# Softmax denominators of 16 attention units by GpSimd, masks by one f16 matmul term in seven units, and a new order of all steps

## The chip, the cores and the metric

The kernel runs on one core of one Trainium2 chip. The metric is the device time of one launch in microseconds (us); lower is better. Five engines work side by side, each through its own instructions in program order: TensorE (PE) multiplies matrices, VectorE (DVE) and ScalarE (ACT) do elementwise work, GpSimd (POOL) does elementwise work and reductions over partitions, and SyncE (SP) starts the transfers between main memory and the on-chip memory. An instruction that waits for another engine holds up everything behind it on its own engine.

## What is computed

Banded attention with block summaries, and then a two-layer MLP with GELU, in float32 (the MLP's weights come as float64). Cut to what matters:

```python
B, H, S, D = 4, 8, 768, 64;  block, window = 32, 16
k_sum = k.reshape(B, H, 24, 32, D).max(axis=3)
v_sum = v.reshape(B, H, 24, 32, D).mean(axis=3)
scores_l = where(|i - j| < window, q @ k.T / 8, -1e9)
scores_s = q @ k_sum.T / 8 + log(block)
a = softmax(concat([scores_l, scores_s]))
x = a @ concat([v, v_sum])                     # 3072 rows x 512
out = gelu(x @ w_in) @ w_out                   # 512 -> 2048 -> 512
```

## The kernel before

**Precision.** A matmul operand is split into two float16 halves, high and low (`..._hi` steps make the high half, `..._lo` steps the rest), and each product is made of three f16 matmuls: high·high, high·low, low·high.

**Tiling.** Attention is cut into 24 units, each 256 queries of four heads of one batch. A unit's scores stand with keys (64 band keys, 24 block summaries, 32 more band keys) on the partitions and 4 × 256 queries along the free axis, a tile of 128 × 1024. Two units (all eight heads) give one chunk of 256 rows for the MLP, 12 chunks in all. Chunks 0 to 3 run the first layer plainly (`phase1 c i`, 24 matmuls of 256 columns). Chunks 4 to 11 go in pairs with a seven-product scheme of Strassen's kind (`sx_...` and `t_...` prepare the sums of its operands, `product p j m` are the matmuls, `keep` and `h_add` combine them). `gelu`, `g_hi`, `g_lo` and then `phase2 c i` (12 matmuls of 512 columns each), `store` and `put` finish a chunk.

**One unit, step by step.** `load_q`, `load_k`, `load_v`, `load_vs` (transfers; `s_load_vs` is a copy on ACT), splits of q, k and v, `scores` (48 small matmuls into `ps_s`), then one of two ways to mask: units 0 to 3 first put the mask into `ps_s` by matmul (`f_mask`, line 617: two terms, f16 mask times a scaled unit matrix, for each half of 512 columns, so 4 matmuls) and copy the scores out on ACT (`evac`, line 654); units 4 to 23 add an f32 mask on DVE while copying (`add_mask`, line 657). Then `maximum` (POOL, line 665, a reduction over the partitions of 128 × 1024), `shift` (DVE), `exponent` (ACT), the split of the probabilities (`s_p_hi` or `p_hi`, then `p_lo`), and `values` on PE: first the denominators, a matrix of ones times the high and the low half of the probabilities (line 709, four matmuls of 512 columns, written side by side into two halves of the partitions), then 48 small matmuls (line 718). `norm_den` (ACT) copies the denominators, `norm_take`, `norm_rec`, `norm_spread` (DVE) invert them, `norm_mult` scales, `x_hi` and `x_lo` (or the `sx` steps) split the result for the MLP.

**Other steps named below.** `wi_diff` and `v_diff` get the low half of a part of `w_in` or of v on PE (an f32 matmul with a unit matrix, recorded as two, lines 424 and 698, and an f16 one, lines 425 and 699), and `wi_dlo` and `v_dlo` copy it out on ACT; `wi_lo` and `v_lo` get the same on DVE. `wi_bits` and `wo_bits` turn float64 bits into float32 on DVE. `warm k n` (line 778) are n filler matmuls whose result nobody reads. `prep_k` and `prep_v` form the block summaries on DVE.

**Order.** The order of everything is written out by hand in `ORDER`, a list of some 1,500 steps, with each engine's program being the steps that it executes, in that order. The waits between engines follow from the data. So where a step stands in `ORDER` sets what it can hold up: transfers are all issued from SP in the order of the list.

**Buffers.** `ps_s` and `ps_v` are single PSUM tiles, four more PSUM banks rotate. `p_h`, `p_l` and `m32` (the maxima) are single; `s32`, `q32` and `v32` are double (unit u uses number u mod 2). `den0` holds the denominators of units 0 to 7 and serves further units in turn with three more tiles.

Of the kernel before, what the change touches and what calls it, by code (L numbers as in the profile page):

```python
# [74 lines left out]
wi_bits 2 0, k_lo 2, wi_dlo 0 1, evac 1, exponent 0, maximum 1, s_p_hi 0, s_k_hi 3, sum_vt 0, sum_vt 1, sum_vt 2,
mean_vt, f_mask 2, scores 2, shift 1, p_lo 0, wi_bits 2 1, wi_bits 1 0, wi_bits 2 2, wi_bits 1 1, k_lo 3, wi_bits 1 2,
s_load_vs 0, v_hi 0, load_vs 1, v_diff 0 1, v_diff 0 0, evac 2, v_hi 1, v_dlo 0 0, v_dlo 0 1, exponent 1, wi_hi 2 1,
wi_hi 2 0, v_diff 1 1, f_mask 3, values 0, wi_diff 2 0, v_diff 1 0, norm_den 0, load_v 2, load_q 3, load_q 4,
s_load_vs 2, q_hi 3, s_p_hi 1, v_hi 2, norm_take 0, norm_rec 0, norm_spread 0, norm_mult 0, p_lo 1, fetch_w_in 6,
load_v 3, v_dlo 1 0, fetch_w_in 5, fetch_w_in 3, wi_hi 1 1, wi_hi 1 0, v_dlo 1 1, warm 3 2, v_diff 2 0, wi_bits 6 0,  # L80
q_lo 3, wi_bits 6 1, wi_diff 1 1, wi_dlo 1 1, v_dlo 2 0, x_hi 0, s_load_vs 3, maximum 2, wi_bits 6 2, x_lo 0, shift 2,
wi_bits 5 0, values 1, v_diff 2 1, scores 3, wi_diff 2 1, wi_dlo 2 0, v_dlo 2 1, evac 3, wi_diff 1 0, wi_hi 6 1,
norm_den 1, v_hi 3, wi_diff 6 1, wi_dlo 1 0, wi_dlo 2 1, norm_take 1, norm_rec 1, norm_spread 1, norm_mult 1,
v_diff 3 0, v_dlo 3 0, wi_hi 6 0, x_hi 1, v_diff 3 1, wi_diff 6 0, exponent 2, wi_dlo 6 0, wi_bits 3 0, x_lo 1,
phase1 0 0, phase1 0 1, fetch_w_in 4, s_p_hi 2, maximum 3, s_k_hi 5, s_k_hi 4, wi_bits 4 0, shift 3, wi_bits 4 1,
p_lo 2, wi_bits 5 1, wi_bits 4 2, wi_bits 3 1, values 2, wi_dlo 6 1, exponent 3, gelu 0 0, norm_den 2, phase1 0 2,
phase1 0 6, s_p_hi 3, s_q_hi 4, wi_bits 5 2, norm_take 2, wi_bits 3 2, norm_rec 2, wi_hi 4 0, gelu 0 2, wi_diff 4 0,
p_lo 3, norm_spread 2, wi_hi 5 1, wi_hi 5 0, g_hi 0 0, wi_hi 3 1, v_dlo 3 1, g_lo 0 0, load_v 5, fetch_w_out 0,
wo_bits 0 0, load_q 5, fetch_w_in 7, load_v 4, norm_mult 2, wo_bits 0 1, wo_bits 0 2, fetch_w_out 4, gelu 0 1,
wi_bits 7 0, g_hi 0 2, wi_dlo 4 0, wi_hi 3 0, wi_hi 4 1, wi_diff 5 0, gelu 0 6, wi_dlo 5 0, wi_diff 3 1, wi_diff 4 1,  # L90
wi_diff 5 1, wi_diff 3 0, x_hi 2, wi_dlo 3 0, wi_dlo 4 1, wi_bits 7 1, x_lo 2, values 3, wi_dlo 3 1, phase1 0 3,
phase1 0 4, norm_den 3, wo_hi 0, wi_dlo 5 1, wi_bits 7 2, phase1 0 5, norm_take 3, s_load_vs 4, wo_lo 0, norm_rec 3,
norm_spread 3, g_lo 0 2, wo_bits 4 0, norm_mult 3, k_lo 4, gelu 0 4, gelu 0 3, x_hi 3, x_lo 3, g_hi 0 3, wi_hi 7 0,
v_hi 4, wo_bits 4 1, wo_bits 4 2, g_hi 0 6, wo_hi 4, k_lo 5, g_lo 0 3, q_lo 4, g_hi 0 1, gelu 0 5, g_lo 0 1, wo_lo 4,
fetch_w_out 1, s_load_vs 5, wi_lo 7 0, wo_bits 1 0, phase1 1 2, phase1 1 1, phase1 1 6, gelu 1 1, g_hi 0 5, wi_hi 7 1,
g_hi 1 1, wo_bits 1 1, scores 4, phase1 1 0, wo_bits 1 2, g_lo 0 5, g_lo 1 1, wo_hi 1, wo_lo 1, wi_lo 7 1, v_hi 5,
fetch_w_out 2, gelu 1 6, g_hi 1 6, gelu 1 0, g_hi 1 0, g_hi 0 4, wo_bits 2 0, g_lo 1 6, wo_bits 2 1, wo_bits 2 2,
phase1 1 5, phase1 1 3, s_q_hi 5, wo_hi 2, v_lo 5, g_lo 1 0, g_lo 0 6, wo_lo 2, fetch_w_out 3, load_mask, gelu 1 5,
gelu 1 3, gelu 1 2, g_hi 1 3, wo_bits 3 0, phase1 1 7, phase1 0 7, phase1 1 4, phase2 1 1, wo_bits 3 1, g_lo 0 4,
wo_bits 3 2, g_hi 1 2, g_lo 1 2, q_lo 5, gelu 1 4, wo_hi 3, load_v 7, load_q 6, s_q_hi 6, fetch_w_out 5, fetch_k 1 0,  # L100
wo_lo 3, wo_bits 5 0, g_lo 1 3, q_lo 6, wo_bits 5 1, wo_bits 5 2, gelu 0 7, gelu 1 7, g_hi 1 5, g_hi 1 4, g_hi 0 7,
wo_hi 5, add_mask 4, maximum 4, wo_lo 5, prep_k 1 0, g_lo 1 4, load_q 7, fetch_w_out 6, wo_bits 6 0, wo_bits 6 1,
fetch_w_out 7, wo_bits 6 2, wo_hi 6, shift 4, exponent 4, wo_lo 6, v_lo 4, load_v 6, wo_bits 7 0, g_lo 0 7,
wo_bits 7 1, phase2 0 1, phase2 1 0, phase2 0 3, phase2 1 2, phase2 0 0, phase2 0 2, phase2 0 4, phase2 0 5, scores 5,
s_p_hi 4, wo_bits 7 2, p_lo 4, wo_hi 7, wo_lo 7, values 4, phase2 0 6, norm_den 4, g_hi 1 7, store 0 0, fetch_v 1 0,
fetch_k 1 1, load_q 8, load_k 6, add_mask 5, g_lo 1 5, maximum 5, prep_v 1 0, norm_take 4, prep_k 1 1, shift 5,
load_k 7, s_k_hi 6, s_k_hi 7, g_lo 1 7, norm_rec 4, prep_k_end 1 0, k_lo 6, norm_spread 4, exponent 5, s_p_hi 5,
put 0 0, fetch_v 1 1, q_hi 7, p_lo 5, prep_k_end 1 1, norm_mult 4, k_lo 7, phase2 1 3, phase2 1 4, phase2 0 7,
store 0 1, phase2 1 5, k_sums 1 0, x_hi 4, scores 6, values 5, prep_v 1 1, x_lo 4, norm_den 5, k_sums 1 1, phase2 1 6,
phase2 1 7, add_mask 6, norm_take 5, norm_rec 5, norm_spread 5, norm_mult 5, load_k 8, fetch_v 3 0, s_q_hi 8,  # L110
s_k_hi 8, maximum 6, q_lo 8, load_vs 6, put 0 1, x_hi 5, store 1 0, x_lo 5, q_lo 7, shift 6, phase1 2 2, phase1 2 0,
v_hi 6, t_add 1 0, t_add 2 0, v_lo 6, k_lo 8, put 1 0, load_vs 7, load_k 9, fetch_k 2 0, load_q 10, load_k 10,
exponent 6, v_hi 7, store 1 1, v_lo 7, load_v 9, load_q 9, scores 7, phase1 2 1, add_mask 7, scores 8, s_p_hi 6,
q_hi 10, s_k_hi 9, p_lo 6, values 6, phase1 2 4, prep_k 2 0, add_mask 8, gelu 2 0, k_lo 9, gelu 2 2, gelu 2 1,
g_hi 2 1, g_lo 2 1, norm_den 6, g_hi 2 2, load_vs 9, fetch_k 2 1, s_q_hi 9, maximum 7, shift 7, exponent 7, g_hi 2 0,
maximum 8, s_p_hi 7, k_hi 10, norm_take 6, norm_rec 6, norm_spread 6, prep_k 2 1, t_add 0 0, norm_mult 6, g_lo 2 0,
p_lo 7, t_add 0 1, q_lo 10, q_lo 9, phase1 2 3, phase1 2 5, phase1 2 7, g_lo 2 2, values 7, x_hi 6, gelu 2 4,
gelu 2 5, g_hi 2 5, gelu 2 3, load_v 8, load_vs 8, v_hi 8, g_hi 2 4, x_lo 6, k_lo 10, phase1 2 6, phase2 2 1, shift 8,
g_hi 2 3, g_lo 2 3, phase2 2 3, phase2 2 0, gelu 2 7, t_add 0 2, norm_den 7, gelu 2 6, v_hi 9, norm_take 7, v_lo 8,
norm_rec 7, norm_spread 7, g_lo 2 4, prep_k_end 2 1, g_lo 2 5, norm_mult 7, g_hi 2 6, x_hi 7, scores 9, load_k 12,  # L120
put 1 1, load_q 12, fetch_v 2 0, t_add 1 1, x_lo 7, add_mask 9, prep_v 3 0, t_add 3 0, load_k 11, phase1 3 6,
phase1 3 2, exponent 8, g_hi 2 7, s_p_hi 8, maximum 9, k_hi 11, g_lo 2 6, prep_v 2 0, scores 10, gelu 3 6, p_lo 8,
add_mask 10, shift 9, gelu 3 2, phase1 3 0, phase1 3 5, values 8, fetch_v 3 1, load_q 11, load_v 10, fetch_k 3 1,
prep_v 3 1, g_lo 2 7, k_lo 11, t_add 1 2, prep_k 3 1, gelu 3 5, norm_den 8, norm_take 8, norm_rec 8, gelu 3 0,
# [104 lines left out]
def band_summary_attention_gelu_mlp(  # L229
# [117 lines left out]
    def setup():  # L347
        nc.gpsimd.memset(eps, 1e-9)
        nc.gpsimd.memset(ones, 1.0)
# [642 lines left out]
```

## Time and profile before

| | |
|---|---|
| time, median of 3 runs (lowest to highest) | 590.68 us (589.96 to 592.59) |
| the profiled execution: its own time / its span | 591.95 us / 590.2 us |
| PE busy | 582.6 us, 99% |
| DVE busy | 429.4 us, 73% |
| ACT busy | 342.4 us, 58% |
| POOL busy | 120.5 us, 20% |
| moved by DMA | 63.91 MB |

The span runs from the first to the last instruction. Busy times of engines overlap. A matmul's record ends when its last result is out, while the next has long begun: a matmul of 512 columns lasts 379 ns in the rows, but its successor starts well before that. So what a matmul costs the engine is read from the distance between two starts in the timeline, and PE's "busy" says only that it never stood empty.

### The profile page before, as it was taken

What the parts mean: (1) busy time and instruction counts of PE and PEld (TensorE: products, weight loads), DVE (VectorE), ACT (ScalarE), POOL (GpSimd) and SP (SyncE); (2) the same over time, 40 slices, a digit from 0 to 9 for tenths busy, and PEclk for the clock granted to TensorE, in tenths of its full rate; (3) what the DMA queues carried; (4) which work ended last, traced back from release to release, by engine and by line L of the source; (5) the groups of instructions that cost most, each with busy time, mean ns of one, the idle gap of its engine ahead of it and who ended that gap; (6) DMA issues with size and microseconds to landing.
All of it is one profiled execution on the core that took longest, in us unless ns stands there. A gap on an engine that the chain in (4) does not pass through costs nothing.

```text
span 590.2 us, 13402 instructions
## 1 busy us (share of the span) xinstructions
PE 582.6 (99%) x5846; PEld 381.7 (65%) x5846; DVE 429.4 (73%) x543; ACT 342.4 (58%) x515; POOL 120.5 (20%) x77
## 2 busy tenths in 40 slices
...
GB/s 335 272 336 91 292 112 215 204 205 178 204 126 174 234 45 115 66 72 100 45 80 87 71 107 42 98 83 48 63 47 33 1 1 37 19 2 1 36 19 36
DMA packets 27306, 63.91 MB, mean 108 GB/s; under 512 B 2480, under 2 KB 6576, under 8 KB 26672
## 3 DMA queue, kind: packets, MB, share of 16 engines
...
HBM read 54.99 MB, written 6.29 MB: 104 GB/s over the span
## 4 chain that ended last, share of the span: by engine, by line
PE 81%; DVE 9%; ACT 4%; DMA 3%; issue 2%; POOL 1%; SPq 0%; DVEq 0%; ACTq 0%; POOLq 0%
PE bank L816 24%; PE bank L864 11%; PE bank L865 11%; PE bank L866 11%; PE bank L789 4%; PE bank L790 4%; PE bank L791 4%; PE ps_v L718 3%; PE ps_s L648 2%; PE bank L424 2%; PE ps_v L709 2%; PE bank L778 2%; DMA stage<-in_vb_dram 1%; DVE p_l L682 1%; DMA stage<-in_w_out_dram 1%
## 5 line engine op out<-in xcount | busy, mean ns | idle before, releaser
L864 PE MATMUL bank<-w_out_h,gh 128*128 128x512 f16 x368 | 139.6, 379 | 0.0
L865 PE MATMUL bank<-w_out_l,gh 128*128 128x512 f16 x368 | 139.5, 379 | 0.0
L866 PE MATMUL bank<-w_out_h,gl 128*128 128x512 f16 x368 | 139.5, 379 | 0.0
L665 POOL PARTITION_ALL_REDUCE m<-s x24 | 81.7, 3404 | 184.2 <-DVE s L657 99.6
L851 DVE SCALAR_TENSOR_TENSOR gl<-g,gh 128x512 f16<-128x512 f32 x96 | 66.0, 696 | 43.1 <-ACT gh L847 42.9
L816 PEld LDWEIGHTS <-w 128*128 128x128 f16 x640 | 62.3, 98 | 8.8
L866 PEld LDWEIGHTS <-gl 128*128 128x128 f16 x368 | 36.0, 98 | 43.4
L816 PEld LDWEIGHTS <-w_in 128*128 128x128 f16 x576 | 55.9, 98 | 9.8
L864 PEld LDWEIGHTS <-gh 128*128 128x128 f16 x368 | 36.0, 98 | 39.6
L865 PEld LDWEIGHTS <-gh 128*128 128x128 f16 x368 | 36.0, 98 | 38.9
L828 DVE TENSOR_TENSOR g<-bank,late 128x512 f32<-128x512 f32 x48 | 32.9, 685 | 35.5 <-PE bank L816 25.3
L847 ACT ACTIVATE gh<-g 128x512 f16<-128x512 f32 x96 | 57.9, 622 | 0.9 <-PE bank L865 0.2
L789 PE MATMUL bank<-x,w_in 128*128 128x256 f16 x192 | 52.4, 273 | 0.0
L790 PE MATMUL bank<-x,w_in 128*128 128x256 f16 x192 | 52.3, 273 | 0.0
L791 PE MATMUL bank<-x,w_in 128*128 128x256 f16 x192 | 52.3, 273 | 0.0
L822 ACT ACTIVATE late<-bank 128x512 f32<-128x512 f32 x48 | 28.1, 590 | 36.2 <-PE bank L816 27.9
L837 ACT ACTIVATE g<-bank 128x512 f32<-128x512 f32 x48 | 28.0, 593 | 32.9 <-PE bank L791 16.5
L816 PE MATMUL bank<-x,w_in 128*128 128x256 f16 x384 | 46.2, 273 | 0.0
L816 PE MATMUL bank<-x,w 128*128 128x256 f16 x320 | 43.5, 273 | 0.0
L816 PE MATMUL bank<-stage,w 128*128 128x256 f16 x320 | 43.5, 273 | 0.0
L837 ACT ACTIVATE g<-g 128x512 f32<-128x512 f32 x48 | 29.6, 625 | 19.9 <-DVE g L828 19.8
L869 ACT ACTIVATE mask_sb<-bank 128x512 f32<-128x512 f32 x23 | 13.6, 591 | 40.2 <-PE bank L866 36.8
...
## 6 DMA issues: line engine op xcount, KB each, us to landing
...
```

Of the source, the lines that this page charges most:

```text
L665: nc.gpsimd.partition_all_reduce(out_ap=m32, in_ap=self.s32, channels=P, reduce_op=bass_isa.ReduceOp.max)
L789: nc.tensor.matmul(dst, wh, xh, start=(k == 0), stop=False)
L790: nc.tensor.matmul(dst, wh, xl, start=False, stop=False)
L791: nc.tensor.matmul(dst, wl, xh, start=False, stop=(k == NCC - 1))
L816: nc.tensor.matmul(dst, l, r[:, k], start=(first and e == 0 and k == 0 and n == 0), stop=(k == KH - 1 and n == 2), skip_group_check=True,)
L828: nc.vector.tensor_tensor(out=g, in0=acc(p, j, a), in1=hsum[s], op=ALU.add)
L837: nc.scalar.activation(g, h, AF.Gelu, scale=1.0 / (SC_X * SC_WI))
L847: nc.scalar.activation(gh, g_ring.use(f"{c}_{i}", g_uses(c, i)), AF.Copy, scale=SC_G)
L851: nc.vector.scalar_tensor_tensor(out=gl, in0=g_ring.use(f"{c}_{i}", g_uses(c, i)), scalar=SC_G, in1=gh, op0=ALU.mult, op1=ALU.subtract)
L864: nc.tensor.matmul(t, gh[:, f, js], w_out_h[:, f, :], start=(n == 0), stop=False)
L865: nc.tensor.matmul(t, gh[:, f, js], w_out_l[:, f, :], start=False, stop=False)
L866: nc.tensor.matmul(t, gl[:, f, js], w_out_h[:, f, :], start=False, stop=(n == NFC - 1))
```

## The change

- `den` is now a step of its own. Eight units (0 to 4, 6, 7, 10) keep the four ones-matmuls; the other sixteen (5, 8, 9, 11 to 23) use `pden`, GpSimd's reduction over partitions with the operation add over the f32 probabilities, into the same tile `m32` that the maxima use, and `norm_pden`, two copies on ACT of 64 partitions each (the epsilon added).
- `f_mask` has one term instead of two (two matmuls instead of four). The term log(block) is added by `evac`, as a bias per partition. Units 0 to 6 take this way (before: units 0 to 3); `add_mask` runs for 17 units instead of 20.
- `v32` is a single tile instead of two. The output tile `ot` is a tile of its own instead of a second use of the mask's tile.
- `wi_diff`/`wi_dlo` run 11 times instead of 14 and `wi_lo` 5 times instead of 2; `v_diff`/`v_dlo` 6 instead of 8, with `v_lo` for 21 units instead of 20.
- Fillers: 33, 4, 1, 2 (40 matmuls) become 14, 5, 6, 2, 10, 10, 10, 1 (58), all ahead of the first `phase1`.
- Some splits move between ACT and POOL: `q_hi` 12 to 9, `k_hi` 10 to 9, `p_hi` 8 to 7, `p_sx_hi` 11 to 13 steps on POOL, the rest on ACT.
- `ORDER` is new throughout. Its start, old and new, stands in the diff.

```diff
-load_q 0, fetch_k 0 0, k_hi 0, s_q_hi 0, q_lo 0, prep_k 0 0, k_lo 0, prep_k_end 0 0, k_sums 0 0, fetch_w_in 0,
-wi_bits 0 0, wi_bits 0 1, load_m16, load_q 1, fetch_k 0 1, load_eye, load_ind, fetch_vt 1, load_q 2, fetch_vt 0,
-fetch_vt 2, warm 0 33, f_mask 0, s_q_hi 1, scores 0, q_lo 1, wi_bits 0 2, prep_k 0 1, fetch_w_in 2, load_v 0,
...
+fetch_k 0 0, prep_k 0 0, load_q 0, load_q 1, load_m16, fetch_k 0 1, s_q_hi 1, s_k_hi 0, q_hi 0, q_lo 0,
+prep_k_end 0 0, warm 0 14, f_mask 0, k_lo 0, k_hi 1, k_sums 0 0, warm 1 5, scores 0, evac 0, fetch_vt 0, load_eye,
+load_ind, load_q 2, q_lo 1, fetch_vt 2, fetch_vt 1, fetch_w_in 1, load_q 3, load_v 0, fetch_w_in 3, k_lo 1,
...
+wi_diff 0 0, wi_dlo 0 0, wi_diff 2 0, s_k_hi 4, s_p_hi 2, wi_bits 6 0, wi_bits 5 0, wi_bits 6 1, x_lo 1, wi_bits 6 2,
+load_v 3, load_q 4, s_q_hi 4, fetch_w_in 4, p_lo 2, wi_dlo 2 1, wi_hi 6 1, wi_hi 3 1, s_q_hi 5, maximum 3,
+s_load_vs 3, shift 3, wi_lo 3 1, wi_bits 5 1, warm 7 1, phase1 0 1, wi_diff 6 1, den 2, norm_den 2, wi_dlo 2 0,
...
+values 14, phase2 4 5, s_p_hi 15, norm_mult 14, p_lo 15, phase2 4 6, values 15, norm_pden 15, load_v 16, store 4 0,
...
+    NV32 = 1
+    v32 = [const.tile([P, UH * CT, D], F32, name=f"v32_{i}") for i in range(NV32)]
...
+        nc.gpsimd.memset(logb, 0.0)
+        nc.gpsimd.memset(logb[SLOT_SUM : SLOT_SUM + NBLK], LOGB)
...
         def f_mask(self):
             self.masked = True
+            part = mask16_sb[:, self.m0 : self.m0 + CH].unsqueeze(1).broadcast_to([P, 2, CH])
             for i in range(2):
-                half = ps_s[:, i * 512 : (i + 1) * 512]
-                for n in range(2):
-                    step = mask16_sb[:, 2 * NMT * TQ + n * P : 2 * NMT * TQ + (n + 1) * P]
-                    part = mask16_sb[:, n * NMT * TQ + self.m0 : n * NMT * TQ + self.m0 + CH]
-                    nc.tensor.matmul(half, step, part.unsqueeze(1).broadcast_to([P, 2, CH]), start=(n == 0), stop=False)
+                nc.tensor.matmul(
+                    ps_s[:, i * 512 : (i + 1) * 512], mask16_sb[:, NMT * TQ : NMT * TQ + P], part, start=True, stop=False
+                )
...
         def evac(self):
-            nc.scalar.activation(self.s32, ps_s, AF.Copy)
+            nc.scalar.activation(self.s32, ps_s, AF.Identity, bias=logb)
...
+        def den(self):
+            for n, p in enumerate((self.ph, self.pl)):
+                for e in range(2):
+                    nc.tensor.matmul(
+                        ps_v[e * D : (e + 1) * D, QCOLS:], ones, p[:, e * QCOLS : (e + 1) * QCOLS],
+                        start=(n == 0), stop=(n == 1),
+                    )
+
+        def pden(self):
+            nc.gpsimd.partition_all_reduce(out_ap=m32, in_ap=self.s32, channels=P, reduce_op=bass_isa.ReduceOp.add)
+
+        def norm_pden(self):
+            for e in range(2):
+                rows = slice(e * D, (e + 1) * D)
+                nc.scalar.activation(
+                    self.x32[rows], m32[rows, e * QCOLS : (e + 1) * QCOLS], AF.Identity, bias=eps[rows]
+                )
```

In `values` the same four ones-matmuls are taken out; the tile `self.den` is renamed to `self.x32`.

More of the change, by code (lines that the diff above doesn't have):

```diff
@@ L75 @@
[L75 to L124, printed above, removed]
@@ new lines @@
+phase2 1 7, norm_mult 5, put 0 0, load_vs 6, load_k 9, load_k 8, store 0 1, k_sums 1 1, put 0 1, fetch_k 2 0,
+s_q_hi 8, maximum 6, shift 6, scores 7, x_hi 5, v_hi 6, exponent 6, store 1 0, x_lo 5, phase1 2 1, phase1 2 2, v_lo 6,
+load_v 7, k_hi 9, k_hi 8, s_p_hi 6, k_lo 9, p_lo 6, den 6, phase1 2 3, values 6, gelu 2 1, gelu 2 2, norm_den 6,
+gelu 2 3, g_hi 2 1, g_hi 2 2, add_mask 7, maximum 7, k_lo 8, prep_k 2 0, norm_take 6, load_q 9, load_k 10, put 1 0,
+load_vs 7, s_q_hi 9, fetch_k 2 1, t_add 1 0, norm_rec 6, q_lo 8, load_q 10, load_k 11, shift 7, phase1 2 0, scores 8,
@@ new lines @@
+store 1 1, exponent 7, norm_spread 6, g_lo 2 1, add_mask 8, k_hi 10, s_p_hi 7, s_q_hi 10, q_lo 9, prep_k 2 1,
+norm_mult 6, p_lo 7, g_hi 2 3, g_lo 2 3, prep_k_end 2 1, v_hi 7, x_hi 6, t_add 1 1, gelu 2 0, x_lo 6, g_hi 2 0,
+phase1 2 4, phase1 2 5, scores 9, phase1 2 7, maximum 8, s_k_hi 11, den 7, phase1 2 6, g_lo 2 0, shift 8, v_lo 7,
+k_lo 10, values 7, norm_den 7, gelu 2 7, exponent 8, g_hi 2 7, norm_take 7, q_lo 10, norm_rec 7, add_mask 9,
+norm_spread 7, gelu 2 5, norm_mult 7, g_lo 2 2, gelu 2 4, g_hi 2 5, x_hi 7, pden 8, s_p_hi 8, k_lo 11, x_lo 7,
@@ new lines @@
+phase1 3 3, phase2 2 1, phase1 3 5, phase2 2 3, k_sums 2 0, gelu 3 5, v_lo 9, shift 9, prep_k 3 0, q_lo 11,
+fetch_v 2 0, prep_v 2 0, g_lo 3 4, load_v 10, load_vs 10, fetch_v 2 1, exponent 9, g_hi 3 0, s_p_hi 9, s_k_hi 12,
+pden 9, v_hi 10, norm_spread 8, k_lo 12, norm_mult 8, p_lo 9, add_mask 10, g_lo 3 0, prep_v 2 1, norm_pden 9,
+phase2 2 5, phase1 3 7, phase2 2 7, phase2 2 4, gelu 3 3, gelu 3 7, phase1 3 2, values 9, phase2 2 6, scores 11,
+maximum 10, v_lo 10, g_hi 3 3, gelu 3 2, g_hi 3 5, shift 10, exponent 10, g_hi 3 7, k_sums 2 1, phase1 3 6, g_lo 3 3,
@@ new lines @@
+t_add 0 1, g_lo 3 5, t_add 0 2, t_add 0 3, t_hi 0 0, g_hi 3 2, add_mask 11, norm_take 9, norm_rec 9, norm_spread 9,
+g_lo 3 2, t_add 2 2, phase2 3 0, phase2 3 2, s_p_hi 10, load_q 13, q_hi 13, p_lo 10, t_hi 0 1, gelu 3 6, store 2 0,
+p_sx_hi 2 0, maximum 11, den 10, shift 11, norm_mult 9, exponent 11, load_v 11, load_q 14, load_vs 11, norm_den 10,
+sx_lo 2 0, t_lo 0 0, values 10, scores 12, pden 11, s_p_hi 11, s_q_hi 14, norm_take 10, norm_rec 10, put 2 0,
+store 2 1, v_hi 11, norm_spread 10, p_lo 11, product 2 0 1, phase2 3 4, phase2 3 1, norm_mult 10, norm_pden 11,
@@ new lines @@
+product 2 3 4, gelu 5 3, h_add 2 3 3, gelu 4 3, gelu 5 7, g_hi 5 3, v_hi 14, p_lo 13, k_lo 16, phase2 5 5,
+product 2 3 3, phase2 4 1, values 13, exponent 14, g_hi 4 6, g_hi 4 3, pden 14, s_k_hi 17, s_p_hi 14, norm_take 13,
+norm_rec 13, v_lo 14, sx_lo 3 0, g_lo 5 3, add_mask 15, norm_spread 13, norm_mult 13, g_lo 4 3, h_add 2 3 1, g_lo 4 6,
+p_lo 14, load_v 15, load_q 17, load_q 18, load_vs 15, sx_hi 3 1, phase2 4 3, norm_pden 14, v_hi 15, norm_take 14,
+gelu 4 7, g_hi 5 7, g_hi 4 7, scores 16, maximum 15, q_hi 17, phase2 4 0, norm_rec 14, add_mask 16, shift 15, v_lo 15,
```

262 lines of the change are left out of this document (138 added, 124 removed).

## The prediction

> **What bounds the kernel now.** I read the page's busy times first, then the busy time by stage (columns: stretch in us, its length, then busy us and count for PE, PE's weight loads, DVE, ACT, POOL; clock, DMA share, GB/s), and then PE's timeline (start, length, engine, line, operation, count, and in brackets idle time and who ended it).
>
> ```profile
> span 590.2 us, 13402 instructions
> PE 582.6 (99%) x5846; PEld 381.7 (65%) x5846; DVE 429.4 (73%) x543; ACT 342.4 (58%) x515; POOL 120.5 (20%) x77
> ```
>
> ```profile
> 0.00:50.50 50.50, 47.29 (x412) 21.14 (x413) 37.09 (x43) 35.42 (x54) 17.17 (x18) 0.97 0.80 290
> 60.00:240.00 180.00, 179.88 (x1928) 120.28 (x1927) 171.05 (x208) 109.30 (x160) 35.76 (x16) 1.00 0.54 174
> 240.00:380.00 140.00, 138.74 (x1588) 98.63 (x1585) 115.60 (x151) 93.58 (x143) 41.99 (x26) 1.00 0.25 77
> 380.00:587.20 207.20, 207.17 (x1800) 133.42 (x1798) 96.19 (x134) 94.49 (x146) 25.61 (x17) 1.00 0.09 30
> 587.20:590.20 3.00, 0.00 (x0) 0.00 (x0) 0.00 (x0) 0.28 (x1) 0.00 (x0) 1.00 0.07 22
> ```
>
> PE never stands empty for long: 3.2 us idle before 50.5 us, 0.12, 1.26 and 0.03 us in the three long stretches, and a tail of 3.0 us in which the last result is copied and written. So the end is set by what PE has to do, plus its start. DVE comes next: it is 95% busy from 60 to 240 us (171.05 of 180), 83% from 240 to 380 us, under half after that. POOL and ACT have room everywhere. Work taken from PE should therefore come off the time nearly one for one, unless DVE or a chain of waits lets PE run dry.
>
> ```profile
> 0.97 10.24 PE L778 MATMUL bank<-ones 128*64 128x512 f16 x33 [0.97 <-POOL ones L349]
> ...
> 14.12 1.02 PE L617 MATMUL ps_s<-mask_sb 128*128 128x512 f16 x4
> 14.98 1.02 PE L424 MATMUL bank<-w,mask_sb 128*128 128x512 f32 x2
> 15.84 0.38 PE L425 MATMUL bank<-w_in,mask_sb 128*128 128x512 f16 x1
> 16.05 1.02 PE L424 MATMUL bank<-w,mask_sb 128*128 128x512 f32 x2
> ...
> 33.86 0.62 PE L778 MATMUL bank<-ones 128*64 128x512 f16 x2
> 36.16 1.12 PE L698 MATMUL bank<-v,mask_sb 128*128 128x512 f32 x2 [1.68 <-ACT v_lo L703]
> 37.12 0.38 PE L699 MATMUL bank<-v_hi,mask_sb 128*128 128x512 f16 x1
> 37.68 2.08 PE L424 MATMUL bank<-w,mask_sb 128*128 128x512 f32 x2 [0.18 <-ACT v_lo L703]
> 39.55 0.63 PE L425 MATMUL bank<-w_in,mask_sb 128*128 128x512 f16 x1
> 40.11 0.64 PE L709 MATMUL ps_v<-p_h,ones 128*64 128x512 f16 x2
> 40.54 0.64 PE L709 MATMUL ps_v<-p_l,ones 128*64 128x512 f16 x2
> ...
> 50.50 0.27 PE L789 MATMUL bank<-x,w_in 128*128 128x256 f16 x1
> ```
>
> The start is different: 10.24 us of it are fillers, and the first MLP matmul comes at 50.50 us. After the gap of 1.68 us PE also runs slower for a while: the f32 pair at 37.68 takes 1.87 us to the next start, the one at 16.05 and its like 0.86.
>
> **The change part by part.** *Denominators.* What the four ones-matmuls cost is the distance from the first of them to the next line:
>
> ```profile
> 478.00 0.38 PE L866 MATMUL bank<-w_out_h,gl 128*128 128x512 f16 x1
> 478.22 0.38 PE L864 MATMUL bank<-w_out_h,gh 128*128 128x512 f16 x1
> ...
> 480.27 0.41 PE L709 MATMUL ps_v<-p_h,ones 128*64 128x512 f16 x2
> 480.51 0.38 PE L709 MATMUL ps_v<-p_l,ones 128*64 128x512 f16 x2
> 480.72 0.20 PE L718 MATMUL ps_v<-p_h,v_hi 128*64 128x64 f16 x2
> ```
>
> 480.72 - 480.27 = 0.45 us. It is not four times the 0.22 us of one matmul of 512 columns (478.00 to 478.22): the two of a pair run side by side. Sixteen units lose it: 16 × 0.45 = **7.2 us** off PE.
>
> *Mask.* Four matmuls cost 14.98 - 14.12 = 0.86 us, so two cost 0.43. Before 4 × 0.86 = 3.44, after 7 × 0.43 = 3.01: 0.4 us off PE in all, but 1.7 off ahead of the first `phase1` (four units) and 1.3 added after it (three).
>
> *Low halves.* A `wi_diff` costs 16.05 - 14.98 = 1.07 us, a `v_diff` the same three passes. Three and two fewer: 5 × 1.07 = 5.35 us off PE. Counted in the two orders, one `wi_diff` and two `v_diff` of these leave the part before the first `phase1` (3.2 us), two `wi_diff` the part after it (2.1 us).
>
> *Fillers.* 18 more, at 0.215 us each, are 3.9 us of PE time at most. They count only where PE would otherwise have worked: in a wait they are free.
>
> *The start.* Of the 50.50 us, 0.97 is the first wait, 10.24 the 33 fillers, 7 × 0.215 = 1.5 the other seven, 2.25 the other idle time (3.2 less 0.97), and 35.5 the rest. From the rest go 1.7 + 3.2 = 4.9 us of work and the slow clock's excess, (1.87 - 0.86) + (0.56 - 0.21) + (0.43 - 0.22) × 2 = 1.8 us, if the fillers keep PE running: 28.8. With 0.97 and 10.24 + 25 × 0.215 = 15.6 for 58 fillers the first `phase1` would come at 45.4 us. Is the input there by then? The keys are now the first transfer. The rows of what feeds the first scores, before:
>
> ```profile
> 5.80 1.75 DVE L495 TENSOR_REDUCE ks<-w_out_l 128x48 f32<-128x1536 f32 x1 [0.85 <-DMA w_out_l<-in_kp_first_dram]
> ...
> 14.16 3.22 POOL L665 PARTITION_ALL_REDUCE m<-s  x1 [7.61 <-ACT s L654]
> ```
>
> With 19 fillers in place of 33 ahead of `scores 0`, PE is ready at 0.97 + 7.2 + 0.4 = 8.6 us, and what follows the keys (5.8 us, 1.75 us for the block maxima, then the splits) is ready at about 9 (estimate from the DVE row). So unit 0 runs some 3 us ahead of before. I take one more us of idle than none: first `phase1` 4 us earlier, with 0 (weights or v late) and 5.1 as bounds.
>
> *After the start.* 7.2 + 2.1 - 1.3 = 8.0 us less PE work. Against it stand new waits. The groups (mean ns is the last number before the bar's end):
>
> ```profile
> L657 DVE SCALAR_TENSOR_TENSOR s<-mask_sb,ps_s 128x1024 f32<-128x1024 f32 x20 | 24.3, 1215 | 4.4 <-PE ps_s L648 4.2
> L688 DVE SCALAR_TENSOR_TENSOR v_lo<-v,v_hi 128x1024 f16<-128x1024 f32 x20 | 25.5, 1274 | 0.2 <-ACT v_hi L685 0.2
> L385 DVE SCALAR_TENSOR_TENSOR w_in<-w,w_in 128x512 f16<-128x512 f32 x1 | 0.7, 684 | 0.0
> L654 ACT ACTIVATE s<-ps_s 128x1024 f32<-128x1024 f32 x4 | 4.1, 1022 | 3.1 <-PE ps_s L648 2.5 <-DVE p_l L682 0.5
> L724 ACT ACTIVATE den<-ps_v,eps 128x512 f32<-128x512 f32 x12 | 8.3, 688 | 8.1 <-PE ps_v L718 4.8 <-DVE x L749 3.2
> ```
>
> DVE loses three `add_mask` (3.65 us) and gains three `wi_lo` (2.05) and one `v_lo` (1.27): even. ACT gains three `evac` (3.1 us) and sixteen times a second copy in `norm_pden` (at most 16 × 0.69 = 11 us), and loses five copies of low halves; it is 58% busy, so this is hidden, unless a copy queues ahead of a `g_hi` that PE waits for. POOL gains sixteen sums. The trace has the maximum, not the sum, over the same 128 × 1024:
>
> ```profile
> L665 POOL PARTITION_ALL_REDUCE m<-s x24: 3214/3223/4186, 14.2 to 462.2; - x24
> ```
>
> Lowest, middle and highest 3.21, 3.22 and 4.19 us. I take 3.4 for a sum, with bounds 3.2 and twice the middle, 6.4: 16 × 3.4 = 54 us on an engine with 470 us free. The sum needs only the exponentials, so it runs beside `s_p_hi`, `p_lo` and `values`; `norm_take` to `norm_spread` can then be over before `values` ends, which shortens a unit's tail. What is queued behind it on POOL are the next unit's splits and its `maximum`, and `maximum` must now also wait until `norm_pden` has read `m32`.
>
> *One v buffer, and the order.* `load_v` of a unit now waits until `v_lo` of the unit before has read the tile, and since SP issues in order, the loads of q and k, the small v transfers and `put` behind it wait too. In the start a v of 0.5 MB takes about 1.8 us at the 290 GB/s of the first row (estimate), and PE's units lie some 10 us apart there, so I cost it at nothing; without that cover it is 1.8 + 1.05 + 1.27, some 4 us a unit with v's two splits. For the reordered list I take 2.5 us of idle after the start instead of 1.4: 1.1 added, with bounds -1.4 and +6.
>
> Sum: -4 - 8.0 + 1.1 = -10.9 us. The profiled execution took 591.95 us beside its span of 590.2; the span would become 579.3. I take the same difference off the median, 590.68, and forecast **579.7 us**.
>
> **The rivals.** *GpSimd's sums hold DVE off (slower).* What one reduction does to DVE can be seen here (timeline; POOL rows, then DVE rows):
>
> ```profile
> 280.69 3.52 POOL L665 PARTITION_ALL_REDUCE m<-s  x1 [2.16 <-DVE s L670]
> 284.08 1.28 POOL L676 CAST p_h<-s 128x1024 f16<-128x1024 f32 x1
> ```
>
> ```profile
> 283.18 1.28 DVE L851 SCALAR_TENSOR_TENSOR gl<-g,gh 128x512 f16<-128x512 f32 x2
> 284.38 2.06 DVE L451 SCALAR_TENSOR_TENSOR w<-w,w 128x1024 f16<-128x1024 f32 x1
> ```
>
> If a sum kept DVE off for its whole 3.4 us, the four sums of units 5, 8, 9 and 11 would add 13.6 us to the stretch where DVE has 9 us free in 180, all of it in gaps of waits; three or four of the five sums of units 12 to 16 would eat most of the 24 us free in the next. That gives 579.7 + 13.6 + 2 = **595 us**, and it turns the change into a loss from about 2.8 us per sum in the dense stretch (10.9 over four). Against it: the two `g_lo` at 283.18 lie inside the reduction and take 0.64 us each, their usual time. Only the plain cast after it stretches a DVE instruction (2.06 us). Chance 7%. The Trainium skill, page "SBUF — State Buffer", section "SBUF: two separate sides", says that DVE and GpSimd share one pair of ports as an exclusive lock, and that a DVE operation with two SBUF inputs and a GpSimd operation that reads SBUF block each other for the whole instruction. By that rule this rival would be the forecast; the cast's row agrees with it, the reduction's rows do not.
>
> *Unit chains become latency-bound (about even).* Where units lie close (8 to 11), one chain of maximum 3.4, shift 1.2, exponent 1.1, sum 3.4 and its copies 1.4 is 10.5 us through one `m32`. If PE waited 3 us at units 8, 9 and 11 for it, or for v through the single tile, the 8.0 us after the start would be given back: 590.7 - 4 - 8 + 9 = **588 us**. For it: DVE has little room there, and SP issues in order. Against it: units 10 and 7 keep PE's own denominators, and PE has MLP matmuls of the chunk before to put in between. Chance 11%.
>
> *The fillers lie on PE's path.* If the extra 18 delay the start instead of filling waits and the rest comes true: 590.7 - 7.2 - 0.4 - 5.35 + 3.9 = **581.6 us**; inside the forecast's range. *PE stays packed from 45.4 us on*: -5.1 - 8.0 - 1.4 = **576 us**, likewise.
>
> **How the numbers follow.** Forecast with its two variants, 574 to 587 us: 80%; even case, 587 to 591: 11%; slower, around 595: 7%; below 574: 2%. The range, 574 to 588.5, holds the forecast, the bounds of the start (0 to 5.1) and of the idle time (-1.4 to +6), and the lower part of the even case. A measurement of this kernel can tell about 0.5% (3 us) from no change. Faster by more than that, under 587.7: 0.83; within: 0.09; slower: 0.08.
>
> **What would show it.** PE's rows of line 709's successor should count 32 matmuls instead of 96; PE's idle time after the first `phase1` should stay under 4 us; the first `phase1` should start at 45 to 47 us, with no slow f32 pairs before it; POOL should be near 175 us busy with sums of 3.2 to 4.2 us; DVE's `g_lo` should keep its mean of about 0.69 us. Wrong would be: PE gaps ended by DVE or POOL in the stretch from 60 to 240 us, sums much longer than the maxima, or a first `phase1` at 50 us or later.

## The result, and the profile after

The changed kernel takes **621.5 us** (median of 4 runs, 618.56 to 621.78) beside 590.5 us of the kernel before: a ratio of 1.0507, 95% interval [1.0466, 1.0547]. It is 5% slower; the forecast was 579.7 us, at most 588.5.

The page of after, busy times (us, share of the span, instructions) and three groups (count | busy, mean ns of one | idle time before, who ended most of it):

```profile
span 619.4 us, 13320 instructions
PE 588.9 (95%) x5783; PEld 379.7 (61%) x5783; DVE 460.7 (74%) x544; ACT 368.6 (60%) x539; POOL 217.0 (35%) x91
L731 POOL PARTITION_ALL_REDUCE m<-s x16 | 100.9, 6307 | 90.8 <-ACT s L678 90.8
L670 POOL PARTITION_ALL_REDUCE m<-s x24 | 81.4, 3391 | 107.0 <-ACT s L659 65.5
L868 DVE SCALAR_TENSOR_TENSOR gl<-g,gh 128x512 f16<-128x512 f32 x96 | 91.5, 962 | 25.5 <-ACT gh L864 25.5
```

A sum (L731) takes 6.31 us in the mean, a maximum over a tile of the same size (L670) 3.39: I had costed the sum at 3.4. PE has 63 instructions fewer than before and yet is busy 6.3 us longer, and it stands 30.5 us instead of 7.6. `g_lo` (L868) went from 0.69 us (mean before 696 ns) to 0.96.

The time by stage, after (stretch, length, busy us and count of PE, PE's weight loads, DVE, ACT, POOL; granted clock, DMA share, GB/s):

```profile
120.00:240.00 120.00, 110.63 (x1285) 71.10 (x1284) 106.91 (x124) 74.79 (x103) 51.78 (x19) 0.95 0.51 148
240.00:380.00 140.00, 131.82 (x1390) 88.59 (x1385) 123.47 (x139) 93.37 (x136) 76.20 (x27) 0.97 0.25 74
380.00:520.00 140.00, 132.74 (x1318) 86.02 (x1316) 97.03 (x118) 87.86 (x126) 67.65 (x23) 0.98 0.15 45
```

The same stages before (the middle one stands in the prediction):

```profile
120.00:240.00 120.00, 119.88 (x1419) 77.60 (x1418) 114.68 (x142) 71.63 (x100) 31.65 (x15) 1.00 0.53 161
380.00:520.00 140.00, 140.00 (x1363) 92.59 (x1362) 82.33 (x114) 75.69 (x113) 25.61 (x17) 1.00 0.11 35
```

Before, PE was full or nearly so in each; now 7 to 9 us are idle in each, and the clock is down as well. One sum shows how that comes about (timeline of after, all engines; start, length, instruction, in brackets idle time and who ended it):

```profile
180.81 6.11 POOL L731 PARTITION_ALL_REDUCE m<-s  x1 [10.48 <-ACT s L678]
...
181.14 0.69 DVE L757 TENSOR_TENSOR den<-ps_v,dent 128x512 f32<-128x512 f32 x1
...
181.75 4.14 DVE L868 SCALAR_TENSOR_TENSOR gl<-g,gh 128x512 f16<-128x512 f32 x1
...
182.12 0.38 PE L882 MATMUL bank<-w_out_l,gh 128*128 128x512 f16 x1
...
185.82 0.81 DVE L637 TENSOR_TENSOR k_lo<-k,k_hi 128x640 f16<-128x640 f32 x1
...
185.95 0.61 PE L883 MATMUL bank<-w_out_h,gl 128*128 128x512 f16 x1 [3.45 <-DVE gl L868]
...
186.35 0.63 PE L881 MATMUL bank<-w_out_h,gh 128*128 128x512 f16 x1
...
186.78 0.63 PE L882 MATMUL bank<-w_out_l,gh 128*128 128x512 f16 x1
```

While the sum runs, a DVE instruction that reads PSUM (181.14) has its usual 0.69 us. The `g_lo` behind it, with two inputs in SBUF (the on-chip memory that isn't PSUM), ends at 185.89 instead of some 0.68 after its start: it is held until about 4.4 us into the sum, and then runs beside the last part of it. In this trace seven `g_lo` begin between 0.9 and 3.4 us into a sum of 6.11 us, and all seven end 5.08 us into it. PE needs its result and stands 3.45 us. The next matmuls are 0.40 and 0.43 us apart instead of 0.22: PE runs at half clock for some 5 us after the gap (the granted clock is 0.50 from 186 to 191 us). The Trainium skill, page "SBUF — State Buffer", section "SBUF: two separate sides", has the two engines exclude each other for the whole instruction; here the hold covers 4.4 of 6.11 us.

And the waits of after (engine, line, what it waited for: us in all, times, longest):

```profile
ACT stage L736 <- POOL m L731: 27.0, 8, 9.8
...
DVE s L675 <- POOL m L670: 10.9, 8, 3.5
ACT v_hi L690 <- DMA v<-vm: 9.8, 5, 3.1
...
PE bank L883 <- DVE gl L868: 4.9, 3, 3.5
...
ACT den L736 <- POOL m L731: 2.4, 2, 1.8
```

`norm_pden` (L736) holds ACT for 29.4 us in all, and behind it in ACT's order stand `g_hi`, `gelu` and the copies that free PE's banks. This the prediction had as a cost of the copies only.

### The profile page after: what moved, and what is told of

Its sections match the earlier page's. It is cut to its first block, busy times and chain, and to the rows that moved or that the text cites. A ratio compares the mean times of both kernels' runs of the same rounds, so it can differ in the third digit from the quotient of the medians.

```text
span 619.4 us, 13320 instructions
## 1 busy us (share of the span) xinstructions
PE 588.9 (95%) x5783; PEld 379.7 (61%) x5783; DVE 460.7 (74%) x544; ACT 368.6 (60%) x539; POOL 217.0 (35%) x91
## 5 line engine op out<-in xcount | busy, mean ns | idle before, releaser
L883 PE MATMUL bank<-w_out_h,gl 128*128 128x512 f16 x368 | 142.6, 388 | 4.9 <-DVE gl L868 4.9
L881 PE MATMUL bank<-w_out_h,gh 128*128 128x512 f16 x368 | 143.1, 389 | 3.5 <-ACT ot L886 2.2
L882 PE MATMUL bank<-w_out_l,gh 128*128 128x512 f16 x368 | 142.5, 387 | 0.0
L731 POOL PARTITION_ALL_REDUCE m<-s x16 | 100.9, 6307 | 90.8 <-ACT s L678 90.8
L670 POOL PARTITION_ALL_REDUCE m<-s x24 | 81.4, 3391 | 107.0 <-ACT s L659 65.5
L868 DVE SCALAR_TENSOR_TENSOR gl<-g,gh 128x512 f16<-128x512 f32 x96 | 91.5, 962 | 25.5 <-ACT gh L864 25.5
L882 PEld LDWEIGHTS <-gh 128*128 128x128 f16 x368 | 36.8, 100 | 43.1 <-issue 6.7
L881 PEld LDWEIGHTS <-gh 128*128 128x128 f16 x368 | 36.7, 100 | 40.3 <-issue 3.4
L806 PE MATMUL bank<-x,w_in 128*128 128x256 f16 x192 | 52.7, 274 | 0.2 <-ACT g L854 0.2
L807 PE MATMUL bank<-x,w_in 128*128 128x256 f16 x192 | 52.6, 274 | 0.0
L808 PE MATMUL bank<-x,w_in 128*128 128x256 f16 x192 | 52.5, 273 | 0.0
L833 PE MATMUL bank<-x,w_in 128*128 128x256 f16 x384 | 47.7, 276 | 0.5 <-ACT g L854 0.5
```

Of the source, the lines that this page charges most:

```text
L670: nc.gpsimd.partition_all_reduce(out_ap=m32, in_ap=self.s32, channels=P, reduce_op=bass_isa.ReduceOp.max)
L731: nc.gpsimd.partition_all_reduce(out_ap=m32, in_ap=self.s32, channels=P, reduce_op=bass_isa.ReduceOp.add)
L806: nc.tensor.matmul(dst, wh, xh, start=(k == 0), stop=False)
L807: nc.tensor.matmul(dst, wh, xl, start=False, stop=False)
L808: nc.tensor.matmul(dst, wl, xh, start=False, stop=(k == NCC - 1))
L833: nc.tensor.matmul(dst, l, r[:, k], start=(first and e == 0 and k == 0 and n == 0), stop=(k == KH - 1 and n == 2), skip_group_check=True,)
```

## The experiments

Three theories of the loss stood at the start. **Hold**: the sums keep DVE off. **Wait**: ACT stands at `norm_pden` until a sum is over. **Order**: the new order keeps PE less full whatever the sums do. Each kernel is after with the edit shown, unless it says otherwise; ratios are to the kernel before, run alongside (590.5 to 591.1 us).

**All denominators back on PE.** For the sixteen units, `pden` and `norm_pden` go, and `den` stands ahead of `values`, `norm_den` behind it:

```diff
-... s_p_hi 8, ... pden 8, ... norm_pden 8, ... norm_take 8, ... values 8,
+... s_p_hi 8, ... den 8, values 8, norm_den 8, norm_take 8,
```

> The changed kernel with all 24 denominators on PE again (the 16 sums taken out, `norm_pden` becomes `norm_den`, ones-matmuls right ahead of `values`); order, masks, single v tile and fillers stay new. PE has 7.2 us more to do than in the changed kernel. If the sums are to blame, by their hold on DVE or by the wait for them: 583 to 591 us, PE idle after 47 us under 6 us, mean clock back to 0.99. If the new order or the single v tile is to blame: 605 us or more, with PE gaps of the same kind at the same places.

626.2 us, 1.0585 [1.0524, 1.0646]: no better, with no sum in it. But the edit brings waits of its own:

```profile
DVE dent L744 <- ACT stage L741: 35.2, 8, 8.1
DVE dent L744 <- ACT den L741: 9.4, 5, 3.9
```

DVE now stands 44.6 us for `norm_den`, which has to wait for `values`. In 13 of the sixteen units the new order has `norm_pden` ahead of `values`; `norm_den` has to stand behind it. So this run says that PE's denominators don't fit the new order at this place, and nothing about the sums. The same with two tiles for v and the norm steps placed later was no cure:

> All 24 denominators on PE in the new order as in the first experiment, with two v tiles, and with `norm_take` to `norm_mult` of each unit moved back in the order until PE has had some 2.6 us more after `values`, where nothing forbids it. In the first experiment DVE stood 45 us ahead of `norm_take`. If that wait made it slow: 592 to 605 us, DVE's wait for `norm_den` under 25 us; the run without any denominators' reduction and with two v tiles took 589 us, and 7.2 us of PE work come on top, so a gain over the kernel before is not expected. If the new order cannot carry PE denominators at all: 615 us or more.

622.2 us, 1.0519 [1.0488, 1.0549]: in the range of the second theory, though DVE's wait for `norm_den` fell to 16.2 us. So that wait alone didn't make the first run slow; what did stays open.

**Sums that nobody reads**, added to that first kernel and to the kernel before (there right behind each `exponent`):

```diff
-exponent 8, ...
+exponent 8, pden 8, ...
```

> As the run with all denominators on PE, but the 16 sums still run at their places on GpSimd, and nobody reads what they give. If a sum does its harm by holding DVE off (4.4 us of each 6.1 us, for DVE instructions with two SBUF inputs): as slow as the changed kernel or slower, 612 to 632 us, `g_lo` again with a mean near 0.96 us. If the harm is the wait of the normalization for the sum: as the run without sums, within 3 us. If it is the order: 605 us or more in both.

> The kernel before, with 16 sums added (units 5, 8, 9, 11 to 23) right behind `exponent`, into the tile of the maxima; nobody reads them, nothing else changes. Hold theory: 16 x 4.4 us of possible hold on a DVE that is 95% busy between 60 and 240 us: 605 to 630 us, DVE busy up by 20 us or more. Wait theory: only `maximum` queues behind a sum: 590 to 598 us. Order theory: 590 to 594 us.

652.0 us, 1.104 [1.0992, 1.1087], and 673.6 us, 1.1404 [1.137, 1.1439]: 26 and 82 us more for sums whose results are not used, and above the ranges given for the hold. No one waits for the result, so holding and GpSimd's own queue do it; these two runs don't tell them apart. In the old order the next unit's maximum is late behind the sum, and DVE with it:

```profile
DVE s L676 <- POOL m L668: 36.2, 7, 13.2
PE bank L822 <- DVE g L834: 24.7, 4, 9.2
```

**A maximum in place of the sum, and no reduction at all:**

```diff
-            nc.gpsimd.partition_all_reduce(out_ap=m32, in_ap=self.s32, channels=P, reduce_op=bass_isa.ReduceOp.add)
+            nc.gpsimd.partition_all_reduce(out_ap=m32, in_ap=self.s32, channels=P, reduce_op=bass_isa.ReduceOp.max)
```

> The changed kernel with the maximum in place of the sum in the 16 GpSimd denominators (they become maxima, so the output changes); same place, input, output and readers. The maximum takes 3.2 us instead of 6.1 and lets DVE's two-input instructions through after about 1.75 us instead of 4.4. Hold theory: most of the loss goes, 583 to 597 us, `g_lo` mean near 0.72 us. Wait theory: about half of the loss goes, 595 to 605 us. Order theory: 615 us or more.

> The changed kernel without the 16 reductions (`norm_pden` reads the maxima that stand in the tile, so the output changes); order, masks, single v tile, fillers unchanged, PE's work as in the changed kernel. With maxima in place of the sums it was 593 us, with 9 us of PE gaps between 120 and 240 us. If those gaps come from what is left of the reductions (hold of 1.75 us each and 3.2 us of wait): 578 to 586 us. If they come from the new order or the single v tile: 588 to 594 us.

593.0 us, 1.003 [1.0012, 1.0049], and 590.95 us, 1.0008 [0.998, 1.0036]. Groups of the first:

```profile
L868 DVE SCALAR_TENSOR_TENSOR gl<-g,gh 128x512 f16<-128x512 f32 x96 | 73.5, 776 | 23.9 <-ACT gh L864 23.9
L731 POOL PARTITION_ALL_REDUCE m<-s x16 | 53.1, 3321 | 87.4 <-ACT s L678 87.4
```

So sixteen reductions of 3.3 us, read and waited for, cost 2 us; the further 3.0 us of each sum cost 28.5. And without any, the new order is as fast as the old one, not 11 us faster. Its page and stages:

```profile
span 588.7 us, 13304 instructions
PE 574.9 (98%) x5783; PEld 375.1 (64%) x5783; DVE 429.1 (73%) x544; ACT 366.6 (62%) x539; POOL 115.5 (20%) x75
```

```profile
120.00:240.00 120.00, 111.71 (x1324) 72.78 (x1323) 106.27 (x129) 77.23 (x108) 31.62 (x16) 1.00 0.51 149
240.00:380.00 140.00, 139.86 (x1569) 97.70 (x1568) 113.94 (x155) 105.66 (x156) 38.45 (x23) 1.00 0.27 83
```

PE runs the same 5783 instructions here as in after. So of the 30.7 us between the two spans, 588.9 - 574.9 = 14.0 are slower matmuls, and 30.5 - 13.8 = 16.7 are idle time. Against before, PE's work is 7.7 us less (582.6 to 574.9) and its idle time 6.2 us more (7.6 to 13.8): from 120 to 240 us alone 8.3 us are idle, where it was 0.1 before.

**A sum over half the columns, and both halves as two sums,** of which only the first is read:

```diff
+            half = UCOLS // 2
+            for dst, i in ((m32[:, :half], 0), (pad, 1)):
+                nc.gpsimd.partition_all_reduce(
+                    out_ap=dst, in_ap=self.s32[:, i * half : (i + 1) * half], channels=P, reduce_op=bass_isa.ReduceOp.add
+                )
```

> The changed kernel with the 16 sums over 512 of the 1024 columns only (the other half is read as the maxima left it, so the output changes). If the hold goes with the size: about 3.1 us long, DVE's two-input instructions let through after about 2.2 us, and by a straight line between the maximum (1.75 us hold, 593 us) and the sum (4.4 us, 621 us) 595 to 601 us. If the hold is a fixed cost of the operation add: 610 us or more.

> The changed kernel with each of the 16 sums cut into two sums of 512 columns: the first half is read by the normalization, the second goes to a tile that nobody reads (the output changes). The result is there after 3.3 us, as with half a sum alone (593 us), but GpSimd is taken up, and DVE held, for both halves. Wait theory (the harm is that `norm_pden`, and ACT behind it, wait for a result that comes 2.9 us later): 592 to 600 us. Hold theory (DVE's two-input instructions are kept off during both halves): 606 to 622 us.

593.4 us, 1.0031 [0.9998, 1.0065], and 614.3 us, 1.0388 [1.0351, 1.0426]. The groups of the second:

```profile
L873 DVE SCALAR_TENSOR_TENSOR gl<-g,gh 128x512 f16<-128x512 f32 x96 | 82.4, 868 | 23.5 <-ACT gh L869 23.5
L734 POOL PARTITION_ALL_REDUCE m<-s x16 | 53.3, 3328 | 90.2 <-ACT s L679 90.2
L734 POOL PARTITION_ALL_REDUCE pad<-s x16 | 57.6, 3601 | 0.0
```

The half sum alone came out a little below its range. In the second kernel the result is there after 3.3 us, as with the half sum, and ACT waits about as little (9.8 us instead of 29.4); the second halves, which nobody reads, cost 20.9 us by holding DVE and keeping GpSimd from other work (6.9 us for both halves, where the whole sum takes 6.3).

**The wait without the hold:** a maximum and six fills of 0.54 us that read nothing, once with `norm_pden` waiting for the last of them, once not:

```diff
+            for _ in range(NPAD):
+                nc.gpsimd.memset(pad, 1.0)
+            nc.gpsimd.tensor_copy(out=m32[:, 0:1], in_=pad[:, 0:1])
```

(The second kernel is without the last line.)

> The run with maxima in place of the sums, and behind each of the 16 a delay on GpSimd of about 2.9 us (six memsets of a tile of their own, which read nothing), on which the normalization then waits: the latency of the sum with the hold of the maximum (the output changes). If the harm of the sum is its hold on DVE: within 5 us of the 593 us of the maxima. If it is the wait for a result that comes 2.9 us later: 610 to 622 us, as the changed kernel.

> The run with maxima in place of the sums, and behind each of the 16 six memsets (3.5 us) of a tile of their own that nobody waits for: GpSimd is taken up as long as by the sums, but the result is there after 3.2 us and DVE is held no longer than by the maxima (the output changes). Occupied-GpSimd theory (what stands behind on GpSimd, the next `maximum` and the splits, comes 3.5 us later): 608 to 622 us. If the wait of the normalization was the harm in the run with the read delay, and the hold in the run with the two halves: 592 to 598 us.

619.8 us, 1.0471 [1.0381, 1.0561], and 599.5 us, 1.0157 [1.0127, 1.0186]. Waits of the first:

```profile
ACT stage L741 <- POOL m L736: 32.8, 10, 9.0
...
ACT den L741 <- POOL m L736: 7.9, 4, 2.8
```

And its `g_lo`:

```profile
L873 DVE SCALAR_TENSOR_TENSOR gl<-g,gh 128x512 f16<-128x512 f32 x96 | 69.9, 738 | 27.4 <-ACT gh L869 27.4
```

It takes 738 ns, so DVE is held no more than with the maxima (776), and yet the kernel is nearly as slow as after: 40.7 us of ACT's time go into that wait. The second shows what GpSimd's being taken costs by itself: 6.5 us over the kernel with the maxima (593.0); 599.5 lies 1.5 above the range that gave it nothing. Put together, over 593.0: taken 6.5, taken and waited for 26.8, the sum itself 28.5; and a sum with an early result, held and taken, 20.9 over its own base of 593.4. Wait and hold don't add up: either one, with GpSimd taken as long, is enough for most of the loss. The wait is priced too high: the fills' result comes some half a microsecond later than a sum's (3.3 + 6 × 0.54 = 6.5 us and 0.3 for a copy of one column, against 6.3), and ACT waits 40.7 us for it instead of 29.4. By how much is not shown, so the two aren't split exactly.

**The copies later,** behind other work on ACT, just ahead of the next unit's maximum:

```diff
-gelu 2 6, norm_pden 8, load_k 12, ... s_q_hi 11, maximum 9,
+gelu 2 6, load_k 12, ... s_q_hi 11, norm_pden 8, maximum 9,
```

> The changed kernel with each `norm_pden` moved back in the order to just ahead of the first step that needs it (`norm_take` of its unit, or the next reduction into the same tile); units 8, 9, 12, 16, 18, 20 and 22 get 1 to 6 us more of ACT work ahead of it, the others under 1 us. Wait theory: 603 to 615 us, and ACT's waits for GpSimd fall from 29 us to under 18. Hold theory: 617 to 624 us.

629.5 us, 1.0645 [1.0608, 1.0681]. ACT's wait fell to 7.0 us, but the next maximum stands behind the read of `m32`, and `shift` behind it:

```profile
DVE s L676 <- POOL m L671: 18.4, 11, 4.0
```

It lies above the ranges of both theories: the wait went, as the first has it, but the sums kept their hold and brought a late maximum.

**v's transfers.** For the idle 8.3 us of the new order without sums, two tiles for v (the mask goes back into the output tile for that), and then v's loads moved in that kernel, for units 6 to 23 far ahead, or for units 8 to 11 by 20 and 14 steps:

```diff
-    NV32 = 1
+    NV32 = 2
```

> As the run without reductions, with two v tiles again (the output tile shares its memory with the f16 mask, as before the change). If the single v tile costs PE anything: at least 3 us less than the run without reductions, and the waits of `v_hi` for transfers (9.8 us in the changed kernel) go. If the v tile is hidden, as the prediction had it: within 2 us.

> The run without reductions and with two v tiles (589.3 us), with `load_v` and `load_vs` of units 6 to 23 moved ahead in the order, to just behind `v_lo` two units earlier (the output is changed as in that run). `v_hi`'s wait for transfers should fall from 8.4 us to under 2. If the late v is what empties PE between 120 and 240 us: 583 to 586 us, PE idle there under 3 us instead of 6. If it is DVE's and ACT's order there: 588 to 590 us.

> The changed kernel, sums and all, with two v tiles and the loads of v moved ahead in the same way. If the loss is nearly all the sums': 615 to 620 us. If late v and late sums stretch the same chain: under 610 us.

> The kernel with the new order, no reductions and two tiles for v (589.3 us), with the load of v 20 steps of the order earlier and its small transfers 14 steps earlier for units 8 to 11 alone, the dense stretch in which TensorE stood for some 8 us. Leaves out what that kernel leaves out (norm_pden reads the maxima, no denominators are summed). If late v is what empties TensorE there: 585 to 587.5 us, and ACT's wait of v_hi for v falls from 8.4 us to under 3. If the chain over DVE and ACT is what empties it: 588.5 to 590 us with that wait gone. If the queue of transfers is disturbed again as in the run with the loads far ahead: over 592 us.

Two tiles: 589.3 us, 0.9964 [0.9938, 0.999]. Far ahead: 627.3 us, 1.0615 [1.0566, 1.0665], and with the sums 659.9, 1.1165 [1.1096, 1.1233]. A little ahead: 588.1 us, 0.995 [0.9932, 0.9968]. The chain of waits of the kernel without sums and with one tile shows what a v costs there (start, length, step):

```profile
171.66 1.14 DVE v_lo L693
...
174.03 4.42 DMA v<-in_vw_dram
...
179.34 7.44 DMA v<-vm
...
186.89 1.06 ACT v_hi L690
```

From the read of one v to the split of the next it is 15.2 us (171.66 to 186.89), 11.9 of them transfers. Moved far ahead, the loads stand in SP's queue until the tile is free, and everything behind them waits too. Waits of SP's queue, and of POOL, in that kernel:

```profile
SPq L591 <- DVE v_lo L693: 176.4, 18, 17.3
```

```profile
POOL k_hi L625 <- DMA k<-in_kd_dram: 80.1, 5, 43.8
```

So that run tells nothing of v itself. The small move does: ACT's wait for v falls from 16.1 us (one tile) over 8.4 (two) to 3.1, and the time by 1.7 and 1.2 us (each step alone is near the noise; both together, 2.9 us, are not). By the first of these expectations the single tile counts as hidden, since two tiles gain less than 2 us. One gap of PE, here in the kernel with one tile, is gone with two:

```profile
215.22 0.27 PE L806 MATMUL bank<-x,w_in 128*128 128x256 f16 x1 [2.48 <-ACT g L854]
```

Five others stay where they were, here in PE's timeline of the last kernel:

```profile
132.25 0.39 PE L883 MATMUL bank<-w_out_h,gl 128*128 128x512 f16 x1 [0.72 <-DVE gl L868]
148.55 0.27 PE L807 MATMUL bank<-x,w_in 128*128 128x256 f16 x1 [1.14 <-DVE x L766]
175.30 0.38 PE L881 MATMUL bank<-w_out_h,gh 128*128 128x512 f16 x1 [1.27 <-ACT g L854]
190.79 0.22 PE L717 MATMUL ps_v<-p_h,v_lo 128*64 128x64 f16 x2 [1.02 <-DVE v_lo L693]
229.73 0.22 PE L717 MATMUL ps_v<-p_h,v_hi 128*64 128x64 f16 x2 [1.68 <-ACT stage L741]
```

They make 5.8 us, ended by DVE and ACT steps of the units and of the MLP. What makes those late wasn't taken apart further; it stays open. The result lies a little below the range of the theory that the chain does it, and above that of late v: both have a part, v 2.9 us.

**Less work for PE in the old order.** One-term masks alone; the denominators from the high halves only, two matmuls instead of four; and both:

```diff
-            for n, p in enumerate((self.ph, self.pl)):
-                for e in range(2):
-                    nc.tensor.matmul(
-                        ps_v[e * D : (e + 1) * D, QCOLS:], ones, p[:, e * QCOLS : (e + 1) * QCOLS],
-                        start=(n == 0), stop=(n == 1),
-                    )
+            for e in range(2):
+                nc.tensor.matmul(
+                    ps_v[e * D : (e + 1) * D, QCOLS:], ones, self.ph[:, e * QCOLS : (e + 1) * QCOLS],
+                    start=True, stop=True,
+                )
```

> The kernel before with one part of the change alone: one-term masks and the bias in `evac` for its units 0 to 3, order untouched. PE has 4 x 0.43 = 1.7 us less to do, all of it before the first `phase1`. If PE's work in the start sets the time: 1.7 us less (589.0). If the start waits for transfers, DVE or ACT anyway: 0 to 0.5 us less.

> The kernel before, order untouched, with the denominators from the high halves of the probabilities alone: two of the four ones-matmuls in each of 24 units go (the low halves are left out of the denominators). PE has 24 x 0.21 = 5.0 us less to do. If PE's work sets the time in the old order: 585.0 to 586.5 us. If DVE's 95% in the stretch from 60 to 240 us sets it: the units 0 to 9 gain nothing, and 587.5 to 588.5 us are left.

> The kernel before with one-term masks for units 0 to 3 and with denominators from the high halves alone (the low halves are left out of the denominators). One-term masks alone gave 0.7 us of their 1.7. If the two add up: 584.5 to 586 us.

590.2 us, 0.9988 [0.9972, 1.0005]; 586.7 us, 0.9937 [0.9917, 0.9957]; 586.0 us, 0.9929 [0.9913, 0.9945]. The last beats both kernels, the one before by 0.7%, some 4.5 us. Its page:

```profile
span 584.1 us, 13293 instructions
PE 574.5 (98%) x5790; PEld 377.7 (65%) x5790; DVE 427.1 (73%) x543; ACT 342.3 (59%) x515; POOL 121.2 (21%) x79
```

PE is as little busy as in the new order without sums (574.9 us), and stands 9.6 us instead of 13.8. So in an order that keeps PE fed, most of the work taken from it comes off the time: 4.5 of the 6.7 us expected (1.7 and 5.0). The denominators then lack the low halves of the probabilities, what f16 rounds away.

## Why the prediction was wrong

The forecast is missed by 621.5 - 579.7 = 41.8 us (its own sum, 590.68 - 10.9, gives 579.8). The kernel without reductions splits that: 30.5 us are the sums (621.5 - 590.95), 11.3 the rest (590.95 - 579.7).

- **The sum's price, the step that failed.** "I take 3.4 for a sum ... on an engine with 470 us free." At 3.3 us the argument held: sixteen maxima in the sums' place cost 2 us. A sum takes 6.3, which was inside my bounds (up to 6.4), but I carried the upper one only into GpSimd's free time, where it is harmless, and not into the two places where it acts: ACT standing at `norm_pden`, and DVE held. In the sum of the forecast, -4 - 8.0 + 1.1, the reductions stand at nothing; they cost 30.5 us, 28.5 of them for the 3.0 us by which a sum is longer than a maximum. So the range had no case with a long sum.
- **The rival "sums hold DVE off"** had the sign and one of the mechanisms, with 7%. What I held against it was misread: the two `g_lo` at 283.18 began 2.49 us into a maximum, and a maximum holds DVE in its first part only. The row that shows it was in the trace of before, inside the maximum from 14.16 to 17.38 (DVE's timeline):

```profile
14.28 1.83 DVE L504 TENSOR_TENSOR ks<-ks,ks 128x48 f16<-128x48 f32 x1
```

  This step, with two inputs and 48 columns, takes 0.21 us elsewhere; it ended 1.95 us into the maximum. In after, going by the overlap of the timeline's rows, 13 `g_lo` that lie beside a sum take 2.44 us in the mean, 72 beside no reduction 0.70. The size was too small even so (595 us): it left out the wait and the slower clock behind some of the gaps.
- **The rival "chains become latency-bound"** (588 us) had the place, one `m32` and ACT's copies, at a sum of 3.4 us; with the sum's real length the wait is the other cause of the loss, as the run with the fills shows.
- **PE's work** fell, but by less than forecast. 32 ones-matmuls are left in after, as forecast:

```profile
L725 PE MATMUL ps_v<-p_h,ones 128*64 128x512 f16 x16 | 3.6, 402 | 0.0
L725 PE MATMUL ps_v<-p_l,ones 128*64 128x512 f16 x16 | 3.4, 379 | 0.0
```

  But without sums PE is busy 7.7 us less than before, beside 10.85 less by my terms (7.2 + 0.4 + 5.35, and 1.8 of slow clock in the start, less 3.9 of fillers). Where the rest went wasn't taken apart.
- **"2.5 us of idle after the start"** was wrong: without any sum 8.3 us are idle from 120 to 240 us alone. I had costed v's single tile from the 290 GB/s of the start, 1.8 us a load; in the chain above its transfers take 11.9 us. Two tiles and slightly earlier loads give 2.9 us back. The other gaps are those of DVE's and ACT's chains in the stretch where I had noted that DVE is 95% busy, and had still expected PE to stay full.
- **The start** was right to about a microsecond: the first `phase1` comes at 47.51 us (forecast 46.5, before 50.50; PE's timeline of after), and the slow f32 pair ahead of it is gone.

```profile
47.51 0.28 PE L806 MATMUL bank<-x,w_in 128*128 128x256 f16 x1
```

- **That work taken from PE comes off the time** holds for the most part in the old order (3.7 of 5.0 us for the low halves of the denominators), not by itself in the new one.
